# Linformer attention and a gated feed-forward layer on one core: the output weights loaded in two halves, the later weight loads made jobs of a stored order, and a new order

## The chip, the core and the metric

The kernel runs on one core of a Trainium2 chip. A core has five engines that run side by side, each through its own list of instructions, in order: TensorE (PE) multiplies matrices and accumulates into the eight banks of PSUM, VectorE (DVE), ScalarE (ACT) and GpSimd (POOL) work on elements, and SyncE (SP) is used here only to issue transfers. Transfers are carried out by 16 DMA engines. An instruction that needs another engine's result, or a landed transfer, waits for a semaphore.

The metric is the device time of one execution in microseconds (us). The kernel before took 518.73 us, the median of three runs that took 518.05, 518.73 and 519.34. The profile is of one further execution.

## The reference

Attention with keys and values projected from 1024 positions to 64 (Linformer), for 8 batches and 8 heads of width 64, and then a gated feed-forward layer (GLU) on its output:

```python
k_proj = np.einsum('ks,bhsd->bhkd', E, k)          # E, F: 64 x 1024
v_proj = np.einsum('ks,bhsd->bhkd', F, v)          # q, k, v: 8 x 8 x 1024 x 64
scores = q @ k_proj^T / sqrt(64)
attn   = softmax(scores)                            # over 64
x      = (attn @ v_proj), heads side by side        # 8192 x 512
out    = (1 / (1 + np.exp(-(x @ w_gate))) * (x @ w_val)) @ w_out
                                                    # w_gate, w_val: 512 x 1536, w_out: 1536 x 512
```

Inputs and output are float32. The kernel works in bf16 on the chip, and its loads convert on the way.

## The kernel before

**Blocks.** The 8192 tokens are 16 blocks of 512, two to a batch; a block's tokens are split in two tiles of 256, a batch's in four. Attention of the first batch (`first_batch`, L784) fills the first 40 us or so, by transposes and copies of its own: `project0` and `turn_k0` for the keys, `h_qt` for the transposes of q on PE, `score`, `lower` (subtracts the maximum), `exp0`, `total0` (row sum), `norm0` (division, L983, operation in L987), `turn_p0` (transpose of the probabilities, copied to `eT`), `project_v0` and `h_xo` (the outputs x, copied to `xT`). From the second batch on q and the outputs are transposed by DMA on SP's queue (`transpose_q`, into `qT`), and a batch's attention is mixed into the feed-forward work of the batch before. `KVs` holds one batch's keys and values, `Qb` its q.

**Feed-forward.** For each block the gate product (x by `wG`) and the value product (x by `wV`) run over chunks of 256 of the 1536 columns, six chunks named by j; `wW[n]` holds gate and value weights. The first block does chunks 0 to 5 plainly: for each 128 columns m (chunk m // 2), four products of 512 columns for the gate and four for the value, one for each 128 rows i of x (`plain_steps` L1035, `mm_one` L1020), and then a tanh on ACT (`tanh0`) and one multiply-add on DVE (`gate0`) that writes `hT`. In `plain_steps` the parameter `cut` says in how many jobs the four products of a bank are issued: for m = 0 and 1 in two, rows 0 and 1 and then 2 and 3, elsewhere in one. The later blocks use a Winograd form of Strassen's scheme with seven products of 256 columns in place of eight, which needs sums of weights (`w_sum` L1098, on POOL or DVE, written to `tG`, `tV` or in place) and of x (`x_sums`, `xS`), snapshots of banks on ACT and adds on DVE.

**Outputs.** The output product (`hT` by `wO`) has the same seven-product form with sums `wT` of the output weights (`o_sum` L1238, four DVE operations, issued at L1250) and sums `hS` of h, on DVE or POOL (`s_sum`). The first and the last block use plain products instead (`o_plain` L1310): four banks of 12 products of 512 columns, one for each 128 rows m of `wO`. `wT` lies in the memory that `pt0` and `xt0` (the first batch's probabilities and outputs) used before; the row `wT<-spare,inv` of the profile at L987 is therefore a normalisation of probabilities.

**Dependences.** `Plan.add` (L65) takes the keys that an operation reads and writes, and makes it wait for the last writers of what it reads and for writers and readers of what it overwrites. A product with the key `"wO"` waits for the load that writes `"wO"`.

**Order.** All work of the steady part is recorded as jobs (an engine, a body, a name) in program order, and then issued by a list that is written out by hand: `ORDER` (L159) holds job numbers, with -1 and -2 for a filler, a product of 256 or 512 columns without use (`busy`, L720), and `PLACES` (L314) holds the bank or the buffer of each job's result in order of recording. Since each engine runs its list in order, `ORDER` is the order of every engine's queue. `run` (L359) reads nothing else: the positions given to `job`, the `release` times, and the tables `AT`, `FB`, `LAND`, `K_AT`, `Q_AT` and `V_AT` move no job (those entries of `FB` and `AT` that begin with `f_` and some others choose engines or forms).

**Loads.** POOL issues all loads (L558), SP the transposes and the stores. `start_loads` (L614) issues, before any job: the two matrices E and F on SP; then on POOL the first batch's k and q, v, and all of `wG` and `wV`: chunk 0 in halves of 128 KB (`ih` picks rows 0, 1 or rows 2, 3; first gate, then value), chunks 3 and 1, two q loads of the first batch's second half, chunks 4, 2 and 5. Loads after that are jobs: the second batch's k, q and v (two each, named KV1 or Q and a head group), and `load_o` (L1785), the output weights, 1536 KB in one load.

Of the kernel before, what the change touches and what calls it, by code (L numbers as in the profile page):

```python
# [7 lines left out]
ALU = mybir.AluOpType  # L8
# [4 lines left out]
P = 128  # L13
# [27 lines left out]
    f_pv00=0, f_pv01=0, f_pv10=1, f_pv11=1, f_s00=1, f_s01=1, f_s10=0, f_s11=0, f_n00=0, f_n01=0, f_n10=1,  # L41
# [112 lines left out]
class Job:  # L154
# [5 lines left out]
    0, -2, -1, 1, 2, -2, -2, -2, 14, 3, 4, 15, 12, 5, 6, 13, 16, 22, 17, 7, 23, 18, 19, 8, -2, -1, 24, 34, 9,  # L160
    20, 25, -2, 10, 32, 35, 11, 21, 33, 26, -2, -2, -2, -2, -1, 36, 42, 28, 37, 52, 43, 38, 53, 39, 27, 44, 54,
    29, 30, 45, 40, 59, 55, 31, 46, -2, -2, -1, 56, 41, 60, 57, 47, 48, 58, 169, 61, -2, 50, 49, 119, 62, 168,
    51, 112, 346, 63, 118, 174, 64, 65, 113, 124, 176, 128, 126, 125, 180, 130, 129, 127, 178, 114, 131, 115,
    116, 165, 120, 68, 175, 122, 66, 121, 69, 67, 123, 86, 88, 179, 87, 76, 70, 89, 136, 71, 177, 77, 144, 72,
    140, 181, 78, 73, 90, 79, 74, 96, 167, 152, 146, 164, 91, 142, 148, 154, 97, 75, 138, 153, 92, 132, 93, 155,
    94, 149, 134, 80, 145, 98, 160, 81, 147, 99, 161, 95, 117, 150, 162, 151, 82, 133, 100, 84, 83, 102, 101,
    85, 137, 103, 190, 166, 106, 135, 104, 108, 183, 141, 163, 107, 139, 105, 301, 187, 192, 109, 185, 302, 143,
    198, 110, 214, 111, 199, 182, 278, 170, 215, 262, 189, 303, 200, 171, 263, 216, 184, 191, 202, 201, 173,
    264, 304, 188, 266, 203, 172, 217, 218, 305, 205, 279, 196, 230, 193, 219, 186, 204, 265, 395, 280, 206,
    221, 281, 267, 220, 222, 209, 207, 269, 223, 210, 246, 270, 396, 211, 231, 225, 212, 227, 234, 197, 247,  # L170
    308, 232, 397, 208, 273, 233, 250, 226, 309, 248, 235, 398, 236, 251, 237, 213, 228, 253, 274, 224, 294,
    238, 229, 254, 239, 252, 295, 241, 249, 296, 243, 307, 255, 240, 282, 297, 257, 244, 242, 259, 256, 306,
    537, 298, 258, 283, 299, 245, 260, 285, 531, 156, 286, 261, 300, 538, 535, 289, 158, 533, 157, 290, 323,
    159, 332, 314, 310, 315, 337, 319, 429, 311, 194, 312, 316, 313, 324, 317, 426, 320, 430, 318, 333, 325,
    334, 326, 328, 321, 427, 423, 329, 322, 428, 338, 335, 327, 330, 339, 331, 268, 431, 195, 424, 341, 336,
    347, 271, 354, 340, 284, 355, 351, 342, 356, 432, 425, 352, 357, 348, 343, 349, 272, 287, 350, 344, 353,
    288, 345, 359, 366, 433, 363, 275, 367, 532, 539, 291, 434, 534, 368, 549, 360, 358, 276, 361, 369, 546,
    364, 362, 365, 375, 547, 292, 378, 370, 376, 371, 536, 548, 550, 372, 377, 277, 551, 379, 373, 293, 380,
    383, 390, 374, 552, 391, 384, 385, 540, 381, 392, 553, 541, 386, 382, 387, 555, 545, 388, 393, 389, 556,
    415, 394, 499, 416, 515, 417, 500, 418, 435, 516, 501, 436, 503, 542, 502, 519, 517, 504, 439, 520, 518,  # L180
    437, 440, 522, 557, 505, 438, 400, 521, 523, 451, 402, 506, 524, 442, 507, 401, 526, 443, 508, 510, 544,
    441, 554, 511, 512, 543, 446, 452, 513, 528, 447, 444, 453, 399, 455, 419, 445, 448, 529, 456, 483, 421,
    514, 558, 527, 509, 467, 420, 484, 454, 559, 422, 530, 458, 468, 487, 449, 403, 459, 489, 560, 488, 471,
    404, 525, 462, 564, 472, 490, 463, 457, 491, 766, 474, 473, 768, 475, 460, 485, 469, 476, 669, 470, 494,
    486, 480, 670, 478, 450, 492, 464, 479, 770, 671, 481, 477, 685, 461, 409, 482, 493, 672, 686, 495, 406,
    765, 673, 410, 675, 465, 405, 674, 496, 769, 689, 411, 676, 466, 690, 412, 771, 497, 677, 687, 413, 678,
    733, 407, 688, 692, 414, 682, 498, 679, 749, 408, 693, 767, 691, 734, 680, 683, 696, 563, 681, 694, 735,
    561, 750, 772, 695, 736, 751, 697, 773, 565, 737, 752, 684, 774, 738, 566, 583, 753, 567, 740, 584, 569,
    568, 775, 570, 754, 578, 741, 777, 585, 780, 779, 571, 744, 574, 579, 781, 572, 575, 586, 756, 573, 745,
    698, 580, 782, 592, 576, 587, 701, 581, 562, 588, 785, 577, 593, 757, 596, 582, 786, 702, 589, 760, 597,  # L190
    787, 705, 590, 594, 703, 789, 591, 598, 704, 601, 761, 595, 790, 599, 602, 699, 605, 608, 603, 707, 600,
    606, 706, 609, 717, 700, 604, 610, 739, 607, 791, 617, 611, 708, 742, 718, 613, 755, 709, 778, 614, 612,
    618, 719, 615, 619, 721, 743, 758, 616, 746, 722, 720, 620, 712, 621, 625, 759, 783, 622, 713, 626, 623,
    710, 784, 747, 776, 724, 711, 624, 762, 788, 627, 629, 748, 637, 628, 714, 630, 638, 796, 725, 631, 641,
    792, 639, 715, 728, 640, 642, 763, 716, 632, 644, 905, 633, 645, 643, 646, 906, 634, 900, 764, 723, 635,
    793, 726, 647, 636, 867, 729, 803, 868, 665, 883, 648, 902, 804, 730, 667, 869, 666, 731, 805, 668, 870,
    871, 794, 806, 807, 727, 872, 809, 797, 808, 795, 819, 732, 798, 874, 907, 899, 810, 875, 908, 904, 811,
    901, 878, 652, 812, 873, 879, 814, 649, 903, 816, 884, 876, 651, 914, 815, 813, 887, 820, 880, 885, 877,
    881, 821, 888, 817, 823, 835, 799, 824, 909, 886, 836, 822, 890, 912, 826, 801, 891, 851, 839, 650, 889,
    840, 910, 894, 892, 882, 837, 895, 915, 911, 838, 842, 827, 896, 852, 653, 917, 843, 897, 855, 913, 893,  # L200
    853, 856, 830, 854, 858, 831, 841, 859, 846, 800, 857, 898, 802, 847, 862, 860, 916, 825, 918, 654, 828,
    659, 863, 844, 845, 656, 864, 861, 660, 1037, 829, 919, 655, 1038, 848, 661, 1039, 849, 920, 663, 1133,
    1040, 832, 865, 1053, 921, 657, 1041, 833, 1054, 923, 1137, 818, 662, 1057, 850, 1135, 1055, 1042, 922, 924,
    1058, 658, 834, 1044, 1060, 1134, 1045, 1056, 926, 664, 866, 1043, 925, 927, 1138, 1061, 1046, 1101, 928,
    1059, 1102, 1117, 1062, 932, 1047, 933, 1050, 931, 934, 929, 1105, 1051, 1103, 1048, 1063, 1104, 1066, 1049,
    935, 937, 1064, 1136, 936, 1139, 1067, 1118, 1140, 1065, 1119, 938, 1141, 1121, 1120, 1106, 946, 1142, 1122,
    939, 942, 947, 1124, 940, 1143, 943, 1052, 941, 1125, 1108, 948, 1145, 1147, 951, 944, 1148, 1109, 952, 955,
# [167 lines left out]
def bass_linformer_attn__then__ffn_glu_sigmoid_kernel(  # L375
# [11 lines left out]
    B = q.shape[0]  # L387
# [8 lines left out]
    with contextlib.ExitStack() as es:  # L396
# [217 lines left out]
        def start_loads():  # L614
# [18 lines left out]
            for R in range(2):  # L633
                load_q_half(0, 1, R)
# [1271 lines left out]
```

## Time and profile before

| what | us |
|---|---|
| median of three runs | 518.73 |
| the profiled execution | 517.88 |
| its span, first to last instruction | 516.1 |
| ACT busy | 374.3 |
| POOL busy | 169.8 |
| landing of the output weights after their issue | 27.9 |
| median landing of a gate chunk of 256 KB after its issue | 15.8 |

The granted clock of TensorE is 1.000 over the whole span. A row of the page for an engine gives its busy time, the share of the span and the number of instructions. PE's busy time counts matmuls whose ends are modelled, so a busy PE may still lose time between two starts; the start of a matmul is what is measured. In the table by stretches a row begins with the stretch in us, then its length, and then for PE, weight loads, DVE, ACT and POOL the busy time with the number of instructions, the mean granted clock, the share of the DMA engines and GB/s. In a timeline a row is a run of like instructions: the start of the first, the length, engine, line, operation, output<-inputs, shape, count, and in square brackets the engine's idle time before with what ended it.

### The profile page before, as it was taken

The page shows a single profiled execution, that of the slowest core. Times are in us where ns is not written, and L with a number is a line of the kernel's source. Part 1 is how long each engine was busy: PE and PEld are TensorE (multiplying, and loading weights), DVE is VectorE, ACT ScalarE, POOL GpSimd, SP SyncE. Part 2 cuts the span into 40 slices and gives each one's busy share as a digit, 9 for nine tenths or more (in the row PEclk, how much of TensorE's full clock was granted, in tenths as well). Part 3 has the DMA queues.
Part 4 walks back from the last instruction along what each step waited for, and adds up shares of the span by engine and source line. Part 5 has one row for each costly group of instructions (what it writes and reads, how often), then busy time and mean ns, then how long its engine had stood idle before and what let it go on. Part 6 is the DMA issues. An engine that isn't in the chain of part 4 may idle for free.

```text
span 516.1 us, 12124 instructions
## 1 busy us (share of the span) xinstructions
PE 509.8 (99%) x4716; PEld 424.0 (82%) x4719; DVE 437.7 (85%) x849; ACT 374.3 (73%) x714; POOL 169.8 (33%) x196
## 2 busy tenths in 40 slices
PE   8999999999999999999999999999999999999997
PEld 4455868889988899888998888888998889988884
DVE  7779998699987999969997799978989889968771
ACT  1666956888876796768967689777878679686652
POOL 9882004610535033340246113620052502403020
PEclk9999999999999999999999999999999999999999
DMA  9999948896679945994669837797565995430204
GB/s 168 197 198 207 187 63 173 135 206 124 144 143 174 189 91 128 169 175 103 122 147 170 156 104 130 157 180 127 142 99 113 197 193 100 98 89 1 83 2 163
DMA packets 140521, 71.57 MB, mean 139 GB/s; under 512 B 97200, under 2 KB 132272, under 8 KB 140464
## 3 DMA queue, kind: packets, MB, share of 16 engines
q0 software_dynamic: 35904, 29.89, 38.0%
q1 hardware_dynamic: 104560, 40.91, 37.8%
q8 instruction: 37, 0.61, 0.5%
q14 instruction: 20, 0.16, 0.1%
HBM read 60.29 MB, written 16.78 MB: 149 GB/s over the span
## 4 chain that ended last, share of the span: by engine, by line
PE 91%; DMA 3%; POOL 3%; DVE 1%; issue 0%; ACT 0%; POOLq 0%
PE pA L517 46%; PE pF L517 45%; DMA wG<-in_moe_w_gate_dram 3%; POOL KVs L558 1%; POOL wG L558 1%; POOL wV L558 1%; DVE hS L546 1%; POOL Qb L558 1%; DVE hT L1057 0%; DVE ost L1405 0%; DVE xT L877 0%; DVE hT L546 0%; ACT ost L531 0%; DVE tV L546 0%; DVE wV L546 0%
## 5 line engine op out<-in xcount | busy, mean ns | idle before, releaser
L531 ACT ACTIVATE spare<-pF 128x512 f32<-128x512 f32 (+2 forms) x167 | 94.3, 574 | 32.1 <-PE pF L517 22.6
L546 POOL TENSOR_TENSOR hT<-hT,hS 128x512 bf16<-128x512 bf16 x42 | 48.1, 1163 | 173.6 <-PE pA L517 98.6
L531 ACT ACTIVATE spare<-pA 128x512 f32<-128x512 f32 (+2 forms) x146 | 83.7, 586 | 20.3 <-PE pA L517 16.4
L1725 POOL TENSOR_TENSOR KVs<-spare,inv 128x384 bf16<-128x384 f32 (+1 forms) x41 | 29.6, 731 | 84.4 <-DVE topf L1636 35.3
L531 ACT ACTIVATE spare<-spare 128x512 f32<-128x512 f32 x74 | 46.2, 628 | 5.9 <-DVE spare L1147 5.5
L1147 DVE TENSOR_TENSOR spare<-pF,spare 128x512 f32<-128x512 f32 x59 | 40.1, 682 | 9.7 <-PE pF L517 4.8
L1216 DVE SCALAR_TENSOR_TENSOR hT<-spare,pF 128x512 bf16<-128x512 f32 x60 | 40.8, 680 | 7.7 <-PE pF L517 3.7
L517 PE MATMUL pA<-wO,hT 128*128 128x256 bf16 (+1 forms) x336 | 47.2, 280 | 0.0
L1147 DVE TENSOR_TENSOR spare<-pA,spare 128x512 f32<-128x512 f32 x54 | 36.7, 682 | 8.5 <-PE pA L517 6.4
L1216 DVE SCALAR_TENSOR_TENSOR hT<-spare,pA 128x512 bf16<-128x512 f32 x52 | 35.3, 680 | 8.3 <-PE pF L517 4.1
L517 PE MATMUL pF<-wO,hT 128*128 128x256 bf16 (+1 forms) x273 | 41.6, 295 | 0.2
L517 PE MATMUL pF<-xT,wV 128*128 128x256 bf16 (+1 forms) x248 | 39.9, 283 | 0.0
L517 PEld LDWEIGHTS pA<-wO,hT 128*128 128x128 bf16 x336 | 32.8, 98 | 6.6 <-ACT KVs L531 0.2
L517 PE MATMUL pA<-xS,wV 128*128 128x256 bf16 x248 | 37.2, 273 | 0.0
L517 PE MATMUL pA<-xT,wG 128*128 128x256 bf16 (+1 forms) x220 | 35.5, 284 | 0.7 <-DVE xT L877 0.5
L517 PE MATMUL pF<-xS,wG 128*128 128x256 bf16 x232 | 34.1, 272 | 0.0
L517 PEld LDWEIGHTS pF<-wO,hT 128*128 128x128 bf16 x276 | 26.6, 98 | 8.7
L517 PE MATMUL pF<-xS,tV 128*128 128x256 bf16 x224 | 33.6, 273 | 0.0
L517 PE MATMUL pA<-xS,tG 128*128 128x256 bf16 x208 | 31.2, 273 | 0.0
L517 PE MATMUL pF<-xT,wG 128*128 128x256 bf16 (+1 forms) x188 | 30.9, 286 | 0.0
L531 ACT ACTIVATE EF<-pA 128x512 f32<-128x512 f32 (+2 forms) x35 | 19.7, 564 | 14.2 <-PE pA L517 13.3
L517 PEld LDWEIGHTS pF<-xT,wV 128*128 128x128 bf16 x248 | 23.9, 98 | 4.3
(186 smaller groups left out, 1286.3 us busy)
## 6 DMA issues: line engine op xcount, KB each, us to landing
out_dram<-ost SPq DMA_DIRECT2D x63, 256.0 KB, 2.4
KVs<-in_v_dram POOLq DMA_DIRECT2D x15, 512.0 KB, 9.5
KVs<-in_k_dram POOLq DMA_DIRECT2D x14, 512.0 KB, 10.4
Qb<-in_q_dram POOLq DMA_DIRECT2D x14, 512.0 KB, 8.8
wO<-in_moe_w_out_dram POOLq DMA_DIRECT2D x1, 1536.0 KB, 27.9
wG<-in_moe_w_gate_dram POOLq DMA_DIRECT2D x5, 256.0 KB, 15.8
wV<-in_moe_w_val_dram POOLq DMA_DIRECT2D x5, 256.0 KB, 16.4
KVs<-in_k_dram POOLq DMA_DIRECT2D x4, 256.0 KB, 6.3
```

What stands on the lines that cost most here:

```text
L517: lambda e: e.matmul(o, lhsT, rhs, **kw),
L531: lambda e: e.activation(o, i, func, scale=scale),
L546: fn = lambda e: e.tensor_tensor(o, a, b, op)
L558: add("POOL", lambda e: e.dma_start(o, i), r=r, w=w, dma=sem, cost=0.78, nbytes=nbytes)
L1147: lambda e: e.tensor_tensor(PB(b)[:, :] if stay else BF(s), PB(b)[:, :], BF(s), ALU.add),
L1216: lambda e: e.scalar_tensor_tensor(o, y.rearrange("p (j c) -> p j c", j=2), 1.0, x.rearrange("p (j c) -> p j c", j=2), ALU.add, ALU.mult,),
L1725: fn = lambda e: e.tensor_tensor(xto.rearrange("p (g h d) -> p h g d", g=2, h=H)[:, hh[0] : hh[1], :, :], o[:, :, 0:DH].rearrange("p (h g) ...
```

## The change

It does six things.

1. `load_o` takes a half: rows m = 0 to 5 (key `("wO", 0)`) and m = 6 to 11 (`("wO", 1)`), half of the rows each, as two POOL jobs. The readers name the half that they read. The first `o_sum` reads half 0 alone.
2. `o_plain` no longer names the sums `("wT", x)`, so that the first block's outputs wait for `hT` and `wO` alone. They never read the sums.
3. `start_loads` ends with the first halves of chunk 0. All other loads of gate and value weights and the two later q loads are POOL jobs (`later_loads`), one for gate and one for value each, so that `ORDER` says where they stand; `load_w` takes the names.
4. Chunk 3 is loaded in halves as chunk 0 was, and the plain products of both chunks are cut in two jobs.
5. The engine of the first half's normalisations can be chosen for each tile (`f_n0..`); all four stay on DVE.
6. `ORDER` and `PLACES` are new, all through, with 24 fillers for 17 (19 of 512 columns for 13, 5 of 256 for 4), and 2923 jobs for 2902.

In `ORDER` the lists of all engines change. POOL's, from the chunk 0 loads on (V, G: value and gate weights, number: chunk, h0 and h1: its halves; K: loads of the second batch's keys, VV: of its values; Q: its q; Q1: the first batch's second half of q; O: output weights; s: a weight sum; n: a normalisation of the first batch's second half; the two batch loads of each kind are for head groups 0 and 1):

```
before: G0h0 V0h0 G0h1 V0h1 G3 V3 G1 V1 Q1 Q1 G4 V4 G2 V2 G5 V5 | VV VV O s s s s K s s s s Q K n n n n Q
after:  G0h0 V0h0 | V3h1 G3h0 V3h0 G3h1 G0h1 V1 V0h1 Q1 Q1 G1 V4 G4 G2 V5 G5 s s V2 s s s VV s s VV
        n n O(h0) n n s K O(h1) K Q Q
```

PE's list at the start, up to the first output group of the first batch (p: half of a projection of K or V with its head group, tQ, tK, tP: transposes of q, of projected K and of the probabilities, sc: a score, su: a subtraction of the maximum, xo: an output group; a digit after f is a number of fillers):

```
before: pK0 f2 pK0 f3 tQ tK tQ pK1 sc sc pK1 su f2 su tQ f1 tK tQ f5 sc sc tP pV0 su pV0 su tP pV1 f3 xo pV1 tP f1 tP
after:  pK0 f3 pK0 f4 tQ tQ tK f3 pK1 sc sc f1 pK1 su f2 tQ tQ tK su f3 sc f2 tP sc su pV0 pV0 su pV1 tP pV1 f1 xo f5 tP
```

Then the feed-forward products begin. ACT's and DVE's lists and the banks are new in the same way.

The diff, cut to its core:

```diff
-    f_pv00=0, f_pv01=0, f_pv10=1, f_pv11=1, f_s00=1, f_s01=1, f_s10=0, f_s11=0, f_n00=0, f_n01=0, f_n10=1,
+    f_pv00=0, f_pv01=0, f_pv10=1, f_pv11=1, f_s00=1, f_s01=1, f_s10=0, f_s11=0, f_n000=0, f_n001=0, f_n010=0, f_n011=0, f_n10=1,
...
 ORDER = (
-    0, -2, -1, 1, 2, -2, -2, -2, 14, 3, 4, 15, 12, 5, 6, 13, 16, 22, 17, 7, 23, 18, 19, 8, -2, -1, 24, 34, 9,
...
+    16, -2, -2, -2, 17, 18, 5, 19, -2, -2, -2, -1, 30, 28, 31, 20, 0, 21, -2, -2, -1, 22, 29, 1, 38, 32, 4, 39,
...
 PLACES = (
-    0, 2, 4, 1, 3, 1, 5, 0, 6, 1, 0, 2, 2, 0, 3, 2, 4, 3, 2, 0, 1, 0, 1, 5, 5, 0, 5, 0, 4, 8, 5, 9, 0, 1, 7, 0,
...
+    0, 3, 4, 3, 2, 1, 6, 1, 5, 0, 4, 4, 0, 1, 0, 3, 2, 2, 5, 1, 1, 1, 4, 3, 3, 5, 7, 1, 1, 9, 7, 10, 0, 7, 7, 4,
...
-        def load_w(j, ih=None):
+        def load_w(j, ih=None, ns="GV"):
             c = slice(256 * j, 256 * j + 256)
             ii = slice(0, NI) if ih is None else slice(2 * ih, 2 * ih + 2)
-            for n in "GV":
+            for n in ns:
...
             load_w(0, 0)
-            load_w(0, 1)
-            load_w(3)
-            load_w(1)
+
+        def later_loads():
+            def one(f):
+                job("POOL", 0.0, f, name="loadw")
+
+            for j, ih in ((3, 0), (0, 1), (3, 1), (1, None)):
+                for n in "GV":
+                    one(lambda j=j, ih=ih, n=n: load_w(j, ih, n))
             for R in range(2):
-                load_q_half(0, 1, R)
-            load_w(4)
-            load_w(2)
-            load_w(5)
+                one(lambda R=R: load_q_half(0, 1, R))
+            for j in (4, 2, 5):
+                for n in "GV":
+                    one(lambda j=j, n=n: load_w(j, None, n))
...
         job = sched.job
+        later_loads()
...
-                eng = "POOL" if FB[f"f_n{hf}{R}"] > 0 else "DVE"
+                eng = "POOL" if FB[f"f_n{hf}{R}" if hf else f"f_n0{R}{t}"] > 0 else "DVE"
...
-                cut = (0, 2, 4) if m < 2 else (0, 4)
+                cut = (0, 2, 4) if m // 2 in (0, 3) else (0, 4)
...
-                (B12, B11, ALU.subtract, ["wO"]),
-                (B22, T[0], ALU.subtract, ["wO", ("wT", 0)]),
-                (B22, B12, ALU.subtract, ["wO"]),
-                (B21, T[1], ALU.subtract, ["wO", ("wT", 1)]),
+                (B12, B11, ALU.subtract, [("wO", 0)]),
+                (B22, T[0], ALU.subtract, [("wO", 1), ("wT", 0)]),
+                (B22, B12, ALU.subtract, [("wO", 0), ("wO", 1)]),
+                (B21, T[1], ALU.subtract, [("wO", 1), ("wT", 1)]),
...
-                    rhs, k = wO[:, m + H6 * (B[1] == "2"), c : c + 256], "wO"
+                    rhs, k = wO[:, m + H6 * (B[1] == "2"), c : c + 256], ("wO", int(B[1]) - 1)
...
-                            [("hT", blk % 2, m, tt // 2), "wO"] + [("wT", x) for x in range(4) if not m],
+                            [("hT", blk % 2, m, tt // 2), ("wO", m // H6)],
...
-                            [("hT", blk % 2, m, 1), "wO"],
+                            [("hT", blk % 2, m, 1), ("wO", m // H6)],
...
-        def load_o():
+        def load_o(x):
+            mm_ = slice(H6 * x, H6 * x + H6)
             load(
-                wO[:, :, :],
-                moe_w_out.rearrange("(m p) c -> p m c", p=P),
-                ["wO"],
-                "wO",
+                wO[:, mm_, :],
+                moe_w_out.rearrange("(m p) c -> p m c", p=P)[:, mm_, :],
+                [("wO", x)],
+                f"wO{x}",
...
-                nbytes=3 << 20,
+                nbytes=3 << 19,
...
-        job("POOL", AT["wo"], load_o, name="loado")
+        for x in range(2):
+            job("POOL", AT["wo"], lambda x=x: load_o(x), name="loado")
```

## The prediction

> **What bounds the kernel now.** I read the page first: the busy shares of part 1 and, in part 4, the chain that ended last.
>
> ```profile
> PE 509.8 (99%) x4716; PEld 424.0 (82%) x4719; DVE 437.7 (85%) x849; ACT 374.3 (73%) x714; POOL 169.8 (33%) x196
> ...
> PE 91%; DMA 3%; POOL 3%; DVE 1%; issue 0%; ACT 0%; POOLq 0%
> ```
>
> TensorE (PE) is busy for 509.8 of 516.1 us and owns 91% of the chain, so a gain must be a moment in which PE waits. The table by stretches says where there are any (columns: PE, PEld, DVE, ACT, POOL busy, clock, DMA share, GB/s):
>
> ```profile
> 20.00:25.00 5.00, 4.97 (x46) 2.21 (x47) 2.97 (x6) 2.17 (x4) 3.65 (x4) 1.00 1.45 196
> ...
> 45.00:50.00 5.00, 4.47 (x51) 3.20 (x50) 5.00 (x13) 3.89 (x9) 0.00 (x0) 1.00 1.24 209
> 50.00:55.00 5.00, 5.00 (x48) 4.38 (x48) 5.00 (x12) 4.88 (x11) 0.00 (x0) 1.00 1.24 205
> ```
>
> ```profile
> 200.00:220.00 20.00, 19.50 (x180) 16.85 (x178) 18.43 (x34) 13.39 (x27) 7.89 (x10) 1.00 0.82 158
> ```
>
> After 50 us PE is full in every stretch but 200:220 and the tail. So what an order can win lies before 50 us. The timeline of PE gives the single waits (start, length, what ran):
>
> ```profile
> 21.70 0.59 PE L517 MATMUL pF<-xT,wV 128*128 128x512 bf16 x2
> ...
> 34.28 1.90 PE L517 MATMUL pA<-xT,wG 128*128 128x512 bf16 x8 [0.20 <-DMA wG<-in_moe_w_gate_dram]
> ...
> 48.58 1.05 PE L517 MATMUL pA<-xT,wG 128*128 128x256 bf16 x8 [0.53 <-DVE xT L877]
> ...
> 68.57 0.39 PE L517 MATMUL pA<-kpD,qT 128*128 128x128 bf16 x4
> ...
> 70.12 2.54 PE L517 MATMUL pF<-wO,hT 128*128 128x512 bf16 x11
> ```
>
> The first products with gate and value weights start at 21.70. At 34.28 PE waits 0.36 us for a gate chunk (the group before it, four 128-column products at 33.70, issues at 0.0555 us each, so it was through at 33.92). At 48.58 it waits 0.70 us for an x copy (eight products from 47.01 at 0.109 us end at 47.88). The intervals used below are read off such groups: 0.2155 us for 512 columns, 0.109 for 256, 0.0555 for 128.
>
> From 21.70 to the first score of the second batch (68.57) the order before holds 96 products of 512 columns (20.69 us), 164 of 256 (17.88), 56 of 128 (3.11), two projections (0.99 each) and three first-batch output groups (0.35 each): 44.70 us in 46.87. So 2.17 us are lost there: 0.36 and 0.70 as above, 0.2 at 23.93 (next start 24.12), 0.2 at 30.0, the rest in pieces under 0.1.
>
> **The change, part by part.** *Output weights in halves, outputs without their sums.* The first block's output products (Oplain) start at 70.12. The last of the four sums that they waited for is this row:
>
> ```profile
> 59.03 0.95 DVE L1250 TENSOR_TENSOR wT<-wO,wT 128x1536 bf16<-128x1536 bf16 x1
> ```
>
> It ends at 59.98, ten microseconds early, and the one load of the output weights landed at 50.6 (22.74 + 27.9). Removing both waits frees 0 us; the cover is those 10 us. What it allows is to move things: the order now has 20 products of 256 columns fewer and 4 of 128 more before the first score, that is 20 x 0.109 - 4 x 0.0555 = 1.96 us less work, done later instead. That is no gain in itself.
>
> *Weight loads as jobs.* The same bytes go through the same queue. One chunk is cut in two, so two issues are added (0.73 us each from issue to issue on POOL), and one for the output weights. In the first row below an issue runs some 28 us ahead of its landing, so the added issues cost 0 while the queue is that full. From landings 1.34 us apart (256 KB chunks) I take the first halves of chunks 0 and 3 at 19.9 to 22.4 and all of both at 25.7; before, chunk 3 was complete at 24.4. Four blocks of columns (16 products, 3.45 us) can now run on first halves, before 8 (1.72): that covers the 0.2 us at 23.93 and the x copy of the other head group.
>
> *Start.* There are 24 fillers for 17: six of 512 and one of 256 columns more, 6 x 0.2155 + 0.109 = 1.40 us of PE. Three stand before the second half of K: 7.75 + 3 x 0.216 = 8.40, where that product started at 8.17. The two Q transposes go before the K transpose, so the K copy on DVE ends at 11.05 instead of 10.66 and the first scores start at 11.6 (before 11.18). The subtraction of the second tile now stands behind the K transpose of the other head group, 14.7 instead of 13.06; its exp, sum, normalisation and transpose follow, so the second transpose of P comes at 19.2 (18.09), the first output group at 20.4 (19.97), the first weight product at 22.1 (21.70). Cost +0.4; bounds: 0, if loads land later than in this execution, as the fillers allow for, and +1.0.
>
> *Steady part to the first score.* I walked the new order by hand with these intervals, ACT at 0.5 to 0.6 and DVE at 0.34 (bf16 sums), 0.60 (PSUM reads) and 0.87 (output sums) from start to start. PE then waits 0.1 at 23.6, twice 0.1 near 42, 0.5 at 44.2 (the eT copy stands behind four gate instructions on DVE), and nothing at the x copy (0.70 saved) or at a gate chunk (0.36 saved: wG2 is wanted at 35.8, landed by 34.3). With 0.5 of small pieces as before: 1.3 us lost for 2.17, that is -0.87. With +0.4: -0.47 at equal work. Bounds: -1.5 (the 0.5 and the start cost vanish) to +1.5 (one DMA wait, below).
>
> *After that.* Work is the same; the PE work between a producer and its reader is as long or longer in the new order (median from a product to the reuse of the bank that a snapshot frees: 2.29 and 2.76 us for G and V, before 2.07 and 2.07). Before loses 0.9 us there, 0.65 of it at 211.42, behind this:
>
> ```profile
> 209.37 1.99 DVE L546 TENSOR_TENSOR hS<-hS,hT 128x1024 bf16<-128x1024 bf16 x1
> ```
>
> ```profile
> 209.64 1.17 POOL L546 TENSOR_TENSOR xS<-xT,xS 128x512 bf16<-128x512 bf16 x1
> ```
>
> That DVE instruction takes 0.68 elsewhere; here POOL runs a sum of 1.17 inside it. I take half of the 0.9, -0.45; bounds -0.9 and +1.5, as much as one such collision at 1.31 and a little more. The Trainium skill, "SBUF — State Buffer", section "SBUF: two separate sides", says that a DVE op with two SBUF inputs and a GpSimd op lock each other out for the whole instruction; 1.99 - 0.68 = 1.31 against 1.17 agrees. By that rule alone the collision may as well come back elsewhere, and this term is 0.
>
> *Sum.* -0.47 - 0.45 = -0.92 against the profiled execution's 517.88 (span 516.1, 1.8 around it): 516.96. That execution lies 0.85 under the median of the runs, 518.73, from which the sum gives 517.81. I put the forecast between them at 517.4.
>
> **The rivals.** *1, given back: 518.6.* The start costs 0.7, the hand walk misses one wait of 0.6, the later term is 0: -0.87 + 0.7 + 0.6 = +0.4, from both bases 518.3 to 519.1. For it: DVE is 5.00 of 5.00 busy at 50:55 and the walk leaves it little room. Against it: the saved 0.70 is a plain change of place. The claimed removal of the wait plays no part here, as above.
>
> *2, more: 516.1.* Start cost 0, walk's 0.5 absent, all 0.9 gone: -0.87 - 0.5 - 0.9 = -2.3, from the two bases 515.6 to 516.4. For it: the fillers suit loads that land some 0.4 later, and the median runs are slower than this one. Against: three things must go well.
>
> *3, slower: 520.8.* POOL issues the late loads in order. Before, most were issued ahead of the normalisations:
>
> ```profile
> 22.74 1.04 POOL L558 DMA_DIRECT2D wO<-in_moe_w_out_dram  x1
> ...
> 34.30 0.78 POOL L558 DMA_DIRECT2D Qb<-in_q_dram  x1
> 35.08 0.75 POOL L558 DMA_DIRECT2D KVs<-in_k_dram  x1
> 35.83 1.06 POOL L987 TENSOR_TENSOR wT<-spare,inv 128x512 bf16<-128x512 f32 x1
> 39.54 1.04 POOL L987 TENSOR_TENSOR wT<-spare,inv 128x512 bf16<-128x512 f32 x1 [2.65 <-DVE inv L981]
> 40.55 1.05 POOL L987 TENSOR_TENSOR wT<-EF,inv 128x512 bf16<-128x512 f32 x1
> 42.87 1.04 POOL L987 TENSOR_TENSOR wT<-spare,inv 128x512 bf16<-128x512 f32 x1 [1.28 <-DVE inv L981]
> 43.85 0.81 POOL L558 DMA_DIRECT2D Qb<-in_q_dram  x1
> ```
>
> Only the last Q load stood behind them. Now the order is: norm, norm, first half of the output weights, norm, norm, a weight sum, K, second half, K, Q, Q. The norms wait for DVE (2.65 and 1.28 us above). By the walk the first half is issued at 38.9 and the next load at 43.7. A load needs some 3.9 us from issue to first byte (K issued at 1.27, landed at 6.5, of which 1.34 transfer), so they must be out by 39.2 and 43.0: the 28 us of reserve are gone and the queue runs dry for 0.7. Behind the loads stand Q and its transposes:
>
> ```profile
> 55.83 8.69 SPq L1484 DMA_TRANSPOSE qT<-Qb  x4
> ```
>
> They began as Q landed (34.30 + 21.5 = 55.8) and land 5.3 later in the median. Now that Q lands at 58.2 + 0.7, its pair of transposes at some 64.2 and 65.5, and the score wants them at 66.2. Slack is under 1 us; from 1 us of lateness of POOL on, PE loses one for one. If the norms come 5 us late, 4 us go to the score: 517.4 - 0.5 + 4 = 520.9, I write 520.8; from 3.3 us it is slower than before by 0.3%. For it: DVE at 30 to 45 is 4.1 to 4.9 of 5 busy. Against: the norms' sums stand earlier on DVE than the gates. The Trainium skill, "DMA: Bandwidth & Descriptors", section "SWDGE vs HWDGE vs iDMA", adds that GpSimd's descriptor writes are locked out while DVE runs in its two-port mode. No row shows that: the issues at 34.30 and 35.08 took 0.78 and 0.75, beside a busy DVE, for 0.73 elsewhere. By it, six issues would each wait for one DVE op of up to 0.95, 5.7 us in all, and this rival would hold.
>
> *4, slower: 520.4.* DVE meets the first output sum at 49.4 in the walk, the half lands at 46.9; at the second it is 56.0 against 53.2. If the halves land 5 us late, DVE, PE's provider for every bank, stands for 2.5: 517.9 + 2.5.
>
> **How the numbers follow.** Forecast 0.45 (516.4 to 518.4), rival 1 0.14, rival 2 0.13, rival 3 0.19, rival 4 0.09. A measurement of this kernel tells 0.3% (1.56 us) from no change, so the bounds are 517.17 and 520.29. Of the forecast 0.25 lies below 517.17; faster 0.25 + 0.13 = 0.38, same 0.20 + 0.14 = 0.34, slower 0.28. Cutting one in ten off each end gives 515.6 to 521.0; the likeliest case's own range is 516.4 to 518.4.
>
> **What would show it.** In the changed kernel's profile: first weight product near 22.1 and first scores near 11.6 (start); no wait over 0.3 at an x copy or a gate chunk before 50; the second batch's first score near 66.2; issues of the output halves near 39 and 44.5, landings near 47 and 53; output sums at 49 and 56 with no idle DVE before them; PE full after 50. I am wrong if a score waits for qT or kpD by over 1 us, or if PE loses over 2 us after 70.

## The result, and the profile after

The changed kernel takes 528.09 us, the median of four runs (525.9 to 528.43), beside 518.39 for the kernel before in the same session (518.0 to 519.34). The ratio of the two is 1.0176 with a 95% interval of 1.016 to 1.0192: slower, where a small gain was forecast and 521.0 was the upper end of the range. The profiled execution took 528.43, of which the span is 526.5 (before 517.88 and 516.1).

Where does it lose? The page gives the first hint: PE has 3.7 us more busy time and its share of the chain that ended last fell from 91% to 82%, with 10% for transfers.

```profile
PE 513.5 (98%) x4726; PEld 425.5 (81%) x4726; DVE 440.5 (84%) x849; ACT 372.3 (71%) x714; POOL 171.5 (33%) x199
...
PE 82%; DMA 10%; issue 4%; POOL 2%; DVE 1%; ACT 1%; POOLq 0%; ACTq 0%
```

The table by stretches (columns as before: PE, weight loads, DVE, ACT, POOL, clock, DMA share, GB/s) says which part of the kernel that is:

```profile
45.00:50.00 5.00, 5.00 (x50) 3.82 (x48) 5.00 (x12) 4.14 (x9) 2.14 (x3) 1.00 1.22 197
50.00:55.00 5.00, 5.00 (x48) 4.44 (x47) 4.86 (x13) 4.47 (x11) 0.00 (x0) 1.00 1.21 194
110.00:115.00 5.00, 2.61 (x19) 1.70 (x18) 4.51 (x8) 3.09 (x6) 0.00 (x0) 0.88 1.33 203
115.00:120.00 5.00, 5.00 (x37) 3.44 (x34) 1.99 (x4) 2.34 (x4) 0.00 (x0) 0.78 0.68 93
170.00:175.00 5.00, 3.13 (x29) 2.47 (x27) 4.96 (x4) 2.68 (x6) 3.14 (x3) 1.00 1.28 98
200.00:220.00 20.00, 20.00 (x196) 17.77 (x194) 14.85 (x34) 16.00 (x33) 8.83 (x12) 1.00 0.67 109
```

The stretches before 55 are full, as they were to be, and so is 200:220, where the kernel before lost 0.5. PE is now idle in stretches where the kernel before had it full: it works 2.61 us of 110:115, at a lower clock, and 3.13 of 170:175. The timeline of PE names the waits behind 70 us (in brackets the idle time and what ended it; start to start a wait is up to 0.3 longer, because the products before it are pipelined):

```profile
96.73 1.05 PE L519 MATMUL pF<-wO,hT 128*128 128x256 bf16 x8 [0.92 <-POOL hT L548]
...
113.73 3.63 PE L519 MATMUL pF<-KVs,EFT 128*64 128x512 bf16 x16 [2.39 <-DMA KVs<-in_k_dram]
...
174.35 0.61 PE L519 MATMUL pA<-xS,wV 128*128 128x256 bf16 x4 [1.87 <-DVE hT L1226]
...
235.71 2.01 PE L519 MATMUL pA<-KVs,EFT 128*64 128x512 bf16 x16 [0.84 <-issue]
...
245.85 0.62 PE L519 MATMUL pA<-kpD,qT 128*128 128x128 bf16 x8 [1.14 <-DMA kpD<-kpd]
...
326.25 0.35 PE L519 MATMUL pF<-vpD,eT 128*128 128x130 bf16 x3 [0.33 <-DMA eT<-KVs]
...
362.64 1.91 PE L519 MATMUL pF<-KVs,EFT 128*64 128x512 bf16 x15 [0.17 <-DMA KVs<-in_v_dram]
...
392.82 0.35 PE L519 MATMUL pA<-vpD,eT 128*128 128x130 bf16 x3 [0.21 <-DMA eT<-KVs]
```

The operands say what each group is: `KVs,EFT` is a projection of K or V, `kpD,qT` a score, `vpD,eT` an output of attention, `xS` and `xT` belong to the products with weights, `hT` and `hS` to the output products. Measured from start to start these are 1.08, 2.56, 2.03, 1.00, 1.30, 0.49, 0.46 and 0.38 us. Behind the second one PE runs at half clock for 3.4 us (the rows from 113:114 to 117:118 added up):

```profile
113.00:114.00 1.00, 0.27 (x2) 0.25 (x4) 1.00 (x2) 0.23 (x1) 0.00 (x0) 0.88 1.23 206
114.00:115.00 1.00, 1.00 (x6) 0.50 (x4) 0.61 (x2) 0.00 (x0) 0.00 (x0) 0.50 1.66 188
115.00:116.00 1.00, 1.00 (x8) 0.64 (x6) 0.00 (x0) 0.00 (x0) 0.00 (x0) 0.50 1.04 62
116.00:117.00 1.00, 1.00 (x8) 0.36 (x4) 0.00 (x0) 0.00 (x0) 0.00 (x0) 0.50 1.31 208
117.00:118.00 1.00, 1.00 (x9) 0.64 (x8) 0.00 (x0) 0.59 (x1) 0.00 (x0) 0.92 0.91 167
```

The 16 products of that projection take 3.56 us (113.73 to 117.29), for 1.85 where they run at full clock, so 1.7 more. The sum is 11.0. The wait of 0.65 that the kernel before had at 211.4 is not there, which leaves 10.4; from 80 us of PE work to the end the changed kernel falls from some 0.4 us ahead to 10.4 behind, 10.8 in all, so these nine items are the loss but for some 0.4 in small pieces.

Three of the waits are for the keys and values of a later batch. In the kernel before none was. For each batch the trace gives the moment at which the last x of the batch before has landed and so left the memory that the loads fill (`landed_x`), the landing of the last of the four K and V loads, and the moment at which PE wants them:

| batch loaded | 3rd | 4th | 5th | 6th | 7th | 8th |
|---|---|---|---|---|---|---|
| before: last x to last K or V landed | 15.2 | 15.3 | 20.5 | 15.6 | 19.9 | 17.3 |
| before: last x to PE wanting it | 17.8 | 17.4 | 22.7 | 22.4 | 22.0 | 18.4 |
| before: margin | 2.6 | 2.1 | 2.2 | 6.8 | 2.1 | 1.1 |
| after: last x to last K or V landed | 19.8 | 18.8 | 18.0 | 14.7 | 19.4 | 16.9 |
| after: last x to PE wanting it | 17.3 | 23.4 | 17.1 | 18.0 | 19.0 | 18.1 |
| after: margin | -2.5 | 4.6 | -0.9 | 3.3 | -0.4 | 1.2 |

The margins of the kernel before are thin: in five of six batches 1.1 to 2.6 us, about one load of 512 KB (2.5 us from landing to landing). The new order moved projections (5th to 7th batch: 3 to 6 us less between x and projection) and moved loads (3rd batch) without keeping them. How the loads of the third batch stand in POOL's list, first before, then after:

```profile
94.29 0.81 POOL L558 DMA_DIRECT2D KVs<-in_k_dram  x1 [0.50 <-issue]
95.09 1.50 POOL L558 DMA_DIRECT2D KVs<-in_v_dram  x2
...
98.80 0.79 POOL L558 DMA_DIRECT2D KVs<-in_k_dram  x1
...
104.04 1.53 POOL L558 DMA_DIRECT2D Qb<-in_q_dram  x2
```

```profile
94.68 0.81 POOL L560 DMA_DIRECT2D KVs<-in_v_dram  x1 [2.42 <-DMA xT<-KVs]
95.50 1.17 POOL L548 TENSOR_TENSOR hT<-hT,hS 128x512 bf16<-128x512 bf16 x1
96.61 0.78 POOL L560 DMA_DIRECT2D KVs<-in_v_dram  x1
97.38 0.75 POOL L560 DMA_DIRECT2D KVs<-in_k_dram  x1
...
99.24 0.78 POOL L560 DMA_DIRECT2D Qb<-in_q_dram  x1
...
101.15 0.78 POOL L560 DMA_DIRECT2D KVs<-in_k_dram  x1
```

Before: K, two V, two sums of h, K, and then both loads of q. After: V, a sum of h behind the first load, V, K, q, K, q, with sums of x between them. Two things are to be seen. The first load waits for the landing of x until 94.68, and the sum at 95.50, which needs nothing from that load, waits behind it: that is PE's wait at 95.5. And a q load that nobody needs yet goes ahead of the last K load.

### The profile page after: what moved, and what is told of

It reads as the page before. It is cut to its first block, busy times and chain, and to the rows that moved or that the text cites. A ratio compares the mean times of both kernels' runs of the same rounds, so it can differ in the third digit from the quotient of the medians.

```text
span 526.5 us, 12130 instructions
## 1 busy us (share of the span) xinstructions
PE 513.5 (98%) x4726; PEld 425.5 (81%) x4726; DVE 440.5 (84%) x849; ACT 372.3 (71%) x714; POOL 171.5 (33%) x199
## 4 chain that ended last, share of the span: by engine, by line
PE 82%; DMA 10%; issue 4%; POOL 2%; DVE 1%; ACT 1%; POOLq 0%; ACTq 0%
PE pF L519 42%; PE pA L519 40%; DMA KVs<-in_k_dram 4%; DMA KVs<-in_v_dram 3%; DMA eT<-KVs 2%; DMA kpD<-kpd 1%; POOL KVs L560 1%; POOL xS L548 1%; DVE hT L1226 1%; ACT spare L533 0%; DVE spare L1157 0%; ACT KVs L533 0%; ACT kpd L533 0%; POOL Qb L560 0%; POOL KVs L1735 0%
## 5 line engine op out<-in xcount | busy, mean ns | idle before, releaser
L1735 POOL TENSOR_TENSOR KVs<-spare,inv 128x256 bf16<-128x256 f32 (+1 forms) x51 | 37.6, 749 | 129.2 <-DVE hS L548 31.4
L519 PE MATMUL pF<-wO,hT 128*128 128x256 bf16 (+1 forms) x324 | 48.8, 292 | 0.9 <-POOL hT L548 0.9
L519 PE MATMUL pA<-wO,hT 128*128 128x256 bf16 (+1 forms) x288 | 40.2, 281 | 0.0
L519 PE MATMUL pA<-xT,wV 128*128 128x256 bf16 (+1 forms) x200 | 33.8, 290 | 0.0
L519 PE MATMUL pF<-xS,tG 128*128 128x256 bf16 x224 | 33.3, 273 | 0.0
L519 PE MATMUL pF<-xT,wV 128*128 128x256 bf16 (+1 forms) x208 | 33.1, 281 | 0.0
L519 PE MATMUL pA<-xS,wV 128*128 128x256 bf16 x200 | 29.7, 273 | 1.9 <-DVE hT L1226 1.9
L519 PE MATMUL pA<-xT,wG 128*128 128x256 bf16 (+1 forms) x180 | 28.5, 284 | 0.0
L519 PE MATMUL pA<-wT,hT 128*128 128x256 bf16 x216 | 28.1, 272 | 0.0
L1226 DVE SCALAR_TENSOR_TENSOR hT<-spare 128x512 bf16<-128x512 f32 x33 | 26.7, 813 | 0.8 <-ACT spare L533 0.5
```

Source lines behind the costliest of these rows:

```text
L519: lambda e: e.matmul(o, lhsT, rhs, **kw),
L1226: lambda e: e.scalar_tensor_tensor(o, y.rearrange("p (j c) -> p j c", j=2), 1.0, x.rearrange("p (j c) -> p j c", j=2), ALU.add, ALU.mult,),
L1735: fn = lambda e: e.tensor_tensor(xto.rearrange("p (g h d) -> p h g d", g=2, h=H)[:, hh[0] : hh[1], :, :], o[:, :, 0:DH].rearrange("p (h g) ...
```

## The experiments

Two theories were set against each other first. A: the edits that the change names cost nothing, the new order of the later batches does. B: the edits themselves cost. Later runs take the waits of A apart. "K, V, Q" are loads, "s" a sum of h (`sum4`) and "x" a sum of x on POOL.

**All edits, old order.** The new code with `ORDER` and `PLACES` of before; the jobs that are new stand where the load or product that they split stood.

```diff
 POOL's first loads
-G0h0 V0h0 | V3h1 G3h0 V3h0 G3h1 G0h1 V1 V0h1 Q1 Q1 ...
+G0h0 V0h0 | G0h1 V0h1 G3h0 G3h1 V3h0 V3h1 G1 V1 Q1 Q1 ...
...
 all later jobs: order and banks as before, O(h0) and O(h1) side by side
```

> All edits of the change are kept (halves of the output weights, no wait for the sums, weight loads as jobs, chunk 3 cut in halves), but the order and the banks are those of before: the two halves and the halves of chunk 3 stand side by side where one load stood. Theory A (the loss is made by the new order of the later batches, the edits themselves cost nothing): 518.4, within 0.8 of before. Rival B (the edits cost: more and smaller loads, outputs that no longer wait): over 521.

Measured: 518.95 (10 runs), ratio 1.0006 (0.9995 to 1.0017). The edits cost nothing that can be told from 0; theory B falls.

**The sums waited for again.**

```diff
-                            [("hT", blk % 2, m, tt // 2), ("wO", m // H6)],
+                            [("hT", blk % 2, m, tt // 2), ("wO", m // H6)] + [("wT", x) for x in range(4) if not m],
```

> The changed kernel, in which the first block's outputs wait for the four weight sums again; nothing else differs. Theory A: no change, 528.1 within 1.0, because the last sum ends some ten microseconds before the outputs start. Rival B (outputs that run ahead push the later work): at least 1.5 less than the changed kernel.

Measured: 527.17 (525.41 to 529.3), ratio to before 1.0168 (1.0139 to 1.0197), an interval that covers that of the changed kernel. No difference can be told from the scatter, so the wait that the change removed shows as none. This execution also had the wait for K at 111, 2.31 long, but no half clock behind it.

**The third batch's loads.**

```diff
 POOL, third batch
-V s V K x Q x K Q
+s K K V x V x Q Q
```

> The changed kernel with one place of POOL's list reordered: in the third batch (loads from 94.7 on) the sum that stood behind the first waiting load goes ahead of it, and the loads go K, K, V, V, Q, Q instead of V, V, K, Q, K, Q. Theory A: the last K lands near 109 instead of 113.7, PE wants it at 111.06 - 1.08 = 110.0; the waits at 95.5 (1.08) and 111.1 (2.56) and the half clock behind it (1.6) go: 528.1 - 5.2 = 522.9. Rival C (waits only move on to the q transposes and scores): over 526.

Measured: 524.14, ratio 1.0109 (1.0093 to 1.0124): 3.95 less than the changed kernel, for 5.2 expected. The timeline of PE shows that the projection no longer waits:

```profile
109.91 1.92 PE L519 MATMUL pF<-KVs,EFT 128*64 128x512 bf16 x16
111.76 0.61 PE L519 MATMUL pF<-xT,tV 128*128 128x256 bf16 x4
```

The 16 products take 1.85 (109.91 to 111.76) and nothing is in brackets. Small waits came up behind it instead (0.33 at 117.9 and 0.25 at 121.7, where scores want projected K and q), and the K wait of the fifth batch grew from 1.00 to 1.21: theory A in the main, a little of rival C.

**All later loads.** The four loads of K and V ahead of q in every later batch, in the same six places.

```diff
 POOL, loads of the 4th to 8th batch (K and V in the order that they had)
-V V K Q K Q | K V Q V K Q | K V V K Q Q | Q K V K V Q | V K K V Q Q
+K K V V Q Q | K K V V Q Q | K K V V Q Q | K K V V Q Q | K K V V Q Q
```

> As the run before, and the six loads of every later batch in the order K, K, V, V, Q, Q as well, in the places that the six held. Theory A: the K waits at 234.6 (1.0) and 361.9 (0.46) go too, and of the 1.3 at 244.4 (transpose of projected K) some 1.0: 522.9 - 2.4 = 520.5. Rival C (q, now last, is late for its transposes and scores wait instead): 522.9 or more.

Measured: 522.12, ratio 1.007 (1.0055 to 1.0085), 2.0 less than the run before. No projection of a later batch waits any more in its trace; the wait for the transpose of projected K fell from 1.32 to 0.53. So the order of the loads, with the one sum, made 6.0 of the 9.7 us by the medians (by the ratios 1.06 of 1.76%, some 5.5 of 9.1 us). What is left in this trace are waits of 2.04, 0.53, 0.40, 0.42 and 0.24.

**The sum alone.** Of the third batch's edit only the sum, with the loads as in the changed kernel.

```diff
 POOL, third batch
-V s V K x Q x K Q
+s V V K x Q x K Q
```

> The changed kernel in which, in the third batch, the sum on POOL that stood behind the first waiting load goes ahead of it; the loads keep the order V, V, K, Q, K, Q. Theory A: the wait of 1.08 at 95.5 goes, but PE then only arrives 1.08 earlier at the product that needs the last K, which lands as before at 113.7: no gain, 528.1 within 0.8. Rival D (the waits add up one by one): 527.0.

Measured: 526.65, ratio 1.0155 (1.0141 to 1.0169): 1.4 less by the medians, where theory A said 0. The interval overlaps that of the changed kernel, so whether there is a gain is not settled by the times. The trace shows what theory A had missed: with the sum out of the way the second V load is issued 0.8 behind the first instead of 1.9, and the last K lands at 112.3 instead of 113.7 (113.7 also in the run with the sums waited for). Counted from the issue of the first load it is issued 1.2 earlier and lands 1.1 earlier. The wait for K is still there (2.41, and the half clock). POOL's list sets the landing of the last load as well as the bytes do; rival D came nearer with its number, but the waits did not add up one by one as it said.

**POOL's sums beside DVE.** In the changed kernel this is what stood behind the wait of 2.03 at 172:

```profile
169.10 4.59 DVE L1226 SCALAR_TENSOR_TENSOR hT<-spare 128x512 bf16<-128x512 f32 x1
173.62 0.67 DVE L1226 SCALAR_TENSOR_TENSOR hT<-spare,pA 128x512 bf16<-128x512 f32 x1
```

```profile
168.96 0.79 POOL L560 DMA_DIRECT2D Qb<-in_q_dram  x1
169.76 1.18 POOL L548 TENSOR_TENSOR hT<-hT,hS 128x512 bf16<-128x512 bf16 x1
170.88 1.16 POOL L548 TENSOR_TENSOR xS<-xT,xS 128x512 bf16<-128x512 bf16 x1
171.99 1.15 POOL L548 TENSOR_TENSOR hT<-hT,hS 128x512 bf16<-128x512 bf16 x1
```

The DVE operation reads and writes SBUF alone. It takes 4.59 us, for 0.68 elsewhere, and ends 0.55 after the last of POOL's three sums (173.14), which had queued up behind another wait and run back to back. The next DVE operation frees the bank for which PE waits. In the edit three of the sums run on DVE:

```diff
-                eng = "POOL" if (AT[f"x{n}"] if blk > 1 else FB[f"f_xs{blk}"]) > 0 else "DVE"
+                eng = "POOL" if (AT[f"x{n}"] if blk > 1 else FB[f"f_xs{blk}"]) > 0 and blk != 5 else "DVE"
...
+                    e_ = "DVE" if blk == 3 and n == 4 and x else eng
```

> As the kernel with all later loads in the order K, K, V, V, Q, Q (522.12), and three sums near 168, which POOL ran back to back while a DVE operation of 0.8 us took 4.60, run on DVE instead. Theory E (the DVE operation was held off by POOL's three): it takes 0.8 again, PE's wait of 2.04 at 168 goes: 520.1. Rival F (DVE is late there for want of inputs, or becomes too full with three more operations): 521.6 or more.

Measured: 521.02 (519.87 to 524.93), ratio 1.0058 (1.0031 to 1.0085): 1.1 less than 522.12 by the medians, 0.6 by the ratios, and the intervals overlap. The times alone show no gain. The DVE operation and PE's wait behave as theory E says:

```profile
165.90 0.68 DVE L1226 SCALAR_TENSOR_TENSOR hT<-spare 128x512 bf16<-128x512 f32 x1
```

It takes 0.68 and PE has no wait at 168. That the three sums held the operation is shown by this. In this execution another wait grew instead, at a place that the edit does not touch:

```profile
120.23 0.40 PE L519 MATMUL pA<-kpD,qT 128*128 128x128 bf16 x4 [1.98 <-DMA kpD<-kpd]
```

The scores of the third batch wait for the transpose of projected K, which landed 4.9 us after its issue (3.3 with the sums on POOL, where the same wait was 0.24); why it took longer is open. The runs of this kernel also spread more than those of the others.

**New start, old rest.** Is the new start worth what it was said to be? Four kernels take the order of the change up to a job, the seam, and then the order of before, with results of the second part moved to another bank only where they collide (2 or 3 of 906).

```diff
+ORDER = the first 364 jobs of the change, then what is left, in the order of before
```

> All edits; the order and banks of the change for the first 364 jobs (to the first block's output products and the first scores of the second batch, some 70 us), then the order and banks of before. Theory A: the new start is worth what the traces show of it, 0.8 at equal landing of the first loads, and nothing is lost later: 518.5 - 0.8 = 517.7. Rival G (what the start gains is taken back where the second batch's x and the next loads meet): 518.5 or more.

> As the run before, and the sum on POOL that in the kernel before ran inside the DVE operation of 1.99 us at 209.4 runs on DVE. Theory E: that operation takes 0.68 and PE's wait of 0.65 behind it goes: 517.7 - 0.6 = 517.1. Rival F: no change against the run before, or slower, as DVE has one operation of 0.4 more there.

Measured: 520.02, ratio 1.0029 (1.0019 to 1.0039), and with the sum on DVE 520.06, ratio 1.0027 (1.0015 to 1.0038). Both are slower than before. The timeline of PE, first run, shows two waits just behind the seam:

```profile
77.83 1.48 PE L520 MATMUL pA<-wO,hT 128*128 128x256 bf16 x12 [0.30 <-ACT KVs L534]
...
80.92 1.25 PE L520 MATMUL pF<-wO,hT 128*128 128x512 bf16 x5 [1.14 <-ACT KVs L534]
```

From start to start they are 0.47 and 1.30, together more than the start gains. The DVE operation of 1.99 us did not come up in the first of the two kernels either (0.69 at 210.87), so the second edit had nothing to remove. POOL's sum came later there, at 212.53, beside DVE operations that read one operand from a bank of PSUM, and these took 0.69 and 0.68 as elsewhere. Two more seams:

```diff
+ORDER = the first 306 jobs of the change, then the order of before
...
+ORDER = the first 572 jobs of the change with the third batch's loads put right, then the order of before
```

> All edits; order and banks of the change for its first 306 jobs (to some 63 us, before the first block's outputs), then the order of before. The run with the cut at 364 jobs lost 0.47 and 1.30 at 77.3 and 79.6, where outputs wait for a bank that a late exp has to leave, and both lie behind its seam. Theory H (those two waits belong to the seam, the new start itself is worth 0.8): 517.8. Rival G (the gain of the start is taken back later wherever the seam lies): 518.6 or more.

> All edits; order and banks of the change with the third batch's sum and loads put right (as in the run that gave 524.14), for the first 572 jobs, to the third batch's projection near 111; then the order of before. Theory A: what that run still lost against before (5.6) lies behind 111, so nothing of it is left: 518.5 - 0.7 = 517.8. Rival G: 518.6 or more.

Measured: 520.3, ratio 1.0037 (1.0022 to 1.0051), and 520.14, ratio 1.0027 (1.0018 to 1.0036). Rival G has the number in both. The first has two waits at its own seam:

```profile
65.70 0.81 PE L520 MATMUL pA<-wO,hT 128*128 128x256 bf16 x6 [0.84 <-ACT spare L534]
...
70.58 0.40 PE L520 MATMUL pF<-kpD,qT 128*128 128x128 bf16 x4 [1.02 <-DVE hT L1227]
```

The second has only small ones there (0.38 and 0.24), but in both the K load of the fifth batch is 1.4 late at 231; in all four mixed kernels the last transpose of x ahead of it lands 4.4 to 4.8 us after its issue, for 3.1 in the kernel before. Why it does was not settled. What the new start is worth was read from traces alone: PE's lost time (start of a product minus the PE work ahead of it, fillers not counted) at 50 us of work is 15.1, 15.7 and 15.8 in three executions with the old start, and 14.4 to 15.6, mean 14.9, in the nine with the new one that have their seam behind this point: some 0.6 better, with a scatter larger than that. The three of the nine over 15 have a wait of 0.9 to 1.04 near 19.5, in which PE waits for the first batch's last V load; it landed at 20.3 to 20.7 there, and at 19.33 in the profile of the changed kernel.

**The dose in the old order.** If margins of one load decide, then one bad exchange in the good order must cost as much as in the bad one.

```diff
 POOL, third batch, order of before
-K V V s s K x Q Q
+K V V s s Q x Q K
```

> All edits with the order of before (518.95), but in the third batch both q loads go ahead of the last K load. A load of 512 KB takes some 2.5 us, K landed at 109.5 in that run and PE took it at 112: now it lands at 114.5 to 115.3. Theory A: PE waits 2.5 to 3.3, and runs at half clock behind it for 1.6 if the wait is like that of the changed kernel: 521.5 to 523.8. Rival I (q earlier is worth as much as K later, since the scores need both): 519.5 or less.

Measured: 524.8, ratio 1.0119 (1.0094 to 1.0144), 5.85 more than the old order without the swap; the forecast reached to 523.8. PE:

```profile
116.17 3.36 PE L520 MATMUL pF<-KVs,EFT 128*64 128x512 bf16 x16 [4.03 <-DMA KVs<-in_k_dram]
```

The last K was issued at 105.41, landed at 116.1 and PE waited 4.20 from start to start; the group of products took 3.36, where it takes 1.92 at full clock. The q transposes that now could start early gave nothing back. The edit moved two things at once: without it K was issued at 99.45, because its new place also stands behind a sum of x, for which POOL waits. The first K load of this batch, the first to be issued after a pause, took 5.9 us from issue to landing (94.89 to 100.80). With only the later issue the last K would by that have landed at some 111.3, an estimate, and PE wanted it at 112.0. So the wait is put down to the two q loads ahead of it; a run with the later issue alone was not made.

**Two waits of the kernel before.** Nothing of the change, two waits that the profile of before shows.

```diff
 DVE, near 46 us
-tV sum, gate, x copy
+x copy, tV sum, gate
...
-                eng = "POOL" if (AT[f"x{n}"] if blk > 1 else FB[f"f_xs{blk}"]) > 0 else "DVE"
+                eng = "POOL" if (AT[f"x{n}"] if blk > 1 else FB[f"f_xs{blk}"]) > 0 and blk != 6 else "DVE"
```

> The kernel before with two of its own waits taken out and nothing of the change: the x copy for which PE waited 0.70 at 48.6 goes ahead of a weight sum and a gate operation on DVE, and the x sum that POOL ran inside the DVE operation of 1.99 us at 209.4 runs on DVE. Theory E and the single waits of the profile: 518.6 - 0.70 - 0.65 = 517.3. Rival F (DVE, full in both places, is late for something else instead): 518.2 or more.

Measured: 517.8 (11 runs), ratio 0.9982 (0.9973 to 0.9991): faster than both kernels, by 0.95 against the runs of before beside it, where 1.35 was expected. The collision is gone, and the x sum costs 0.41 on DVE:

```profile
210.27 0.69 DVE L546 TENSOR_TENSOR hS<-hS,hT 128x1024 bf16<-128x1024 bf16 x1
...
211.48 0.41 DVE L546 TENSOR_TENSOR xS<-xT,xS 128x512 bf16<-128x512 bf16 x1
```

The operation that took 1.99 takes 0.69, and the stretch around it is 0.9 shorter. The other wait only moved, as rival F said, to a later product that reads a DVE result (0.72 from start to start):

```profile
50.77 0.61 PE L517 MATMUL pA<-xS,tG 128*128 128x256 bf16 x4 [0.56 <-DVE xS L546]
```

## Why the prediction was wrong

*The start and the steady part to the first score: right, with two errors against each other.* First scores at 12.03 (11.6 forecast), first output group at 20.67 (20.4), weight products from 22.4 (22.1), first score of the second batch at 65.93 (66.2). The start cost 0.7 for 0.4 forecast, within its bounds; its first load landed 0.9 later than in the execution of before. From there to the first score PE lost 0.8 (42.74 of work in 43.53) for 1.3 forecast, and the wait of 0.5 expected at 44.2 did not come. At 80 us of work the changed kernel was some 0.4 ahead, for 0.47 forecast.

*The halves: right.* Issues of the output weights and the sums of them, in the timelines of POOL and DVE:

```profile
38.86 0.89 POOL L560 DMA_DIRECT2D wO<-in_moe_w_out_dram  x1
...
44.06 0.83 POOL L560 DMA_DIRECT2D wO<-in_moe_w_out_dram  x1
```

```profile
49.14 0.95 DVE L1260 TENSOR_TENSOR wT<-wO 128x1536 bf16<-128x1536 bf16 x1
...
55.98 0.95 DVE L1260 TENSOR_TENSOR wT<-wO,wT 128x1536 bf16<-128x1536 bf16 x1
```

Issues near 39 and 44.5, sums at 49.4 and 56.0 were forecast. The halves landed at 47.6 and 55.05, for 47 and 53: the second was 2 us later than forecast and 0.9 ahead of its sum. DVE had no wait before either sum. And removing the wait for the sums freed nothing that could be measured, as the run with it put back shows.

*Rivals 3 and 4: did not happen.* The four q transposes landed at 63.97, 65.59, 66.93 and 68.1, and the scores ran without a wait, though the first started only 0.34 behind the second landing:

```profile
65.93 0.39 PE L519 MATMUL pA<-kpD,qT 128*128 128x128 bf16 x4
...
67.26 1.03 PE L519 MATMUL pF<-wO,hT 128*128 128x512 bf16 x4
```

The issues of POOL at 38.86 and 44.06 took 0.89 and 0.83 beside a busy DVE. So the possibility taken from the Trainium skill ("DMA: Bandwidth & Descriptors", section "SWDGE vs HWDGE vs iDMA"), that such issues wait for DVE, finds no support in these rows; in which mode the DVE operations beside them ran, no row shows.

*"After that": the step that failed.* The prediction put this term at -0.45 with bounds of -0.9 and +1.5, on the words that the work is the same and that "the PE work between a producer and its reader is as long or longer in the new order". That was measured on one kind of pair, the banks that snapshots free. Of the moved steps it did not count the DMAs of the later batches: their place in POOL's list, what stands behind a load that waits there, and the PE work from the last x to the projection. The term was +10.8 in the profiled execution. By experiment the order of loads and sums on POOL made 6.0 of the 9.7 between the medians. Without the collision of POOL's sums with a DVE operation a wait of 2.0 went from the trace; what that is worth in time is not shown. The rest, in the traces: 0.49 and 0.38 where outputs of attention wait for transposed probabilities, and what is left of the waits for projected K; that was not tried. Both signs of being wrong that the prediction named came true: a score waited 1.30 for `kpD` at 244.6, and PE lost far more than 2 us after 70.

*The collision.* The term rested on a row in which POOL ran one sum inside a DVE operation, and bounded a new one at 1.31 "and a little more". Three sums in a row held an operation for 3.9 us (4.59 - 0.68): DVE did not get in between the sums of 1.18, 1.16 and 1.15. The collision of before did not come back at 211, but this one came up at 169. The Trainium skill ("SBUF — State Buffer", section "SBUF: two separate sides") has the side that starts first hold the ports for a whole instruction while the other fully blocks. The traces agree on the blocking, but by the rows the DVE operation started first both times, 0.27 and 0.66 ahead of the first sum, and ended 0.55 behind the last. POOL's spans are rough and a load's issue stands right ahead of the sum both times, so who came first stays open.

*The sign.* 0.28 was given to slower, none of it for this reason; both slower rivals were mishaps of the second batch, and their highest price, 4 us, came from one wait. Rival 3 had the right kind of loss, a transfer that is late by its place in POOL's list, and looked for it in one batch of seven.

## What to carry to other kernels

A new order of everything has to be read everywhere: for each transfer of the steady part, from what releases it to who first needs it, against the kernel before. Where a margin is about one load wide, a load that is put ahead of the one that is needed makes PE wait, and half clock behind the wait can add to it. An instruction that waits at the head of a queue makes what stands behind it late, and things that pile up behind it then run back to back and can hold off another engine.

## What was not expected of the hardware

PE's granted clock fell to 0.50 behind waits of 2.41, 2.56 and 4.20 us, and did not behind waits of 2.31, 2.14 and 2.03. In the clock record of the fourteen traces every change lies a whole number of 3.41 us behind the first, and each of the three falls ahead of the last product lasted 3.41 us. Counted in these windows, PE stood idle for 2.41, 2.56 and 3.41 us of the window before the three falls, and for at most 2.1 us of any other window up to the last product; the wait of 2.31 had 2.1 in one window and the rest in the next. So where a wait falls in the windows decides as well as its length, which is luck for a kernel: of the four runs of the changed kernel three show a mean clock of 0.997, and the one of 525.9 shows 1.000. The Trainium skill ("TensorE: Matmul & The Clock Gate", section "Part 1: The HAM clock gate") speaks of an idle window of some 3.4 us. Here 2.41 us of idle time in a window were enough, and the measurement decides; between 2.1 and 2.41 nothing was measured.

From issue to landing the transposes of x took 3.0 to 5.6 us within the changed kernel, and that of projected K ahead of the wait at 244.6 took 5.8 (3.3 for the same batch in the kernel before). The first K load of an execution landed between 6.5 and 7.4 us.
